# Top-k attention with a gated feed-forward layer on one core: token layout, zero matmuls and a reordered opening

## The chip, the cores and the metric

The kernel runs on one core of a Trainium2 chip. Its time is device time in microseconds (us). Three runs of the kernel before gave 1637.67, 1638.57 and 1638.79 us; the median, 1638.57 us, is the time before. One further execution was taken by the hardware profiler: 1636.0 us in all, of which the profile's span covers 1634.2 us. All steps below are read from that execution.

Engines are named as the profile names them: PE multiplies matrices (PEld is its weight load), DVE is the vector engine, ACT the scalar engine with its function tables, POOL the general-purpose engine, SP the engine that issues the DMAs. Each engine works through its own list of instructions in order.

## The reference

```python
# q, k, v: (8, 8, 576, 64)  batch, heads, tokens, head dim
scores = (1/sqrt(64)) * q @ k.T                    # 576 x 576 for each of 64 heads
kth    = 32nd largest of each row of scores
attn   = softmax(where(scores >= kth, scores, -1e9))
x      = (attn @ v), heads side by side            # 4608 x 512
h      = x @ w_in                                  # 512 -> 2048
out    = (h * sigmoid(1.702 h)) @ w_out            # 2048 -> 512
```

The two weight matrices arrive as 64-bit floats, so the kernel also has to turn them into 32-bit floats, piece by piece.

## The kernel before

**Tiling.** For one batch element a *slot* is 128 query rows of a pair of heads (or the 64 left-over rows of two pairs): 18 slots for each of the 8 batch elements, so N is 144. Per slot:

- `prepare` (L185) transposes the loaded q and k of a head pair on PE, and ACT copies them out; this happens once for each pair of heads of a batch element.
- `scores` (L215) multiplies q by k on PE, and ACT copies the 2 x 576 scores of each row to SBUF (tile `sc`, L232).
- `topk` (L234) finds the 32 largest on DVE: 14 operations, eight MAX8 (L241) and six MATCH_REPLACE8 (L244), two at a time for the two heads.
- `bounds` (L255) takes two small steps on POOL; `exponentials` (L263) takes two Prelu (L269) and two Exp steps (L271) on ACT; `divide` (L276) takes the reciprocal of the row sum on DVE. For slots below SETTLED (9) POOL writes diagonal matrices `by` (L286) with it; afterwards ACT and POOL scale the probabilities (L288, L289).
- `turn` (L291) transposes the probabilities on PE (L302, or L300 once settled; L305 for the left-over keys) with ACT copies `pt` (L310); `values` (L322) multiplies by v (L332), and ACT copies the result to `xT` (L344).
- When all four head pairs of a row tile are done, `hidden` (L364) makes a quarter of the hidden layer on PE (32 matmul instructions, L373), `tanh` (L385) runs on ACT, `gate` (L397) on DVE or POOL, and `project` (L411) multiplies by a quarter of w_out (8 matmul instructions of 512 columns, L421).

**Weights.** 32 pieces of 512 KB are loaded (`load_piece`, L113). `round_piece` (L122) turns each into 32-bit floats in steps: *size* on ACT (L142), *shift* on DVE (L143), *low* (L145) and *sign* (L144) on ACT, and *finish*, two POOL instructions (L138 and L139). `by_slot` (L442) says how many pieces each of slots 0 to 8 handles: 4, 3, 3, 4, 3, 4, 3, 4, 4. The finishes of one slot's pieces stand in POOL's list in the next slot.

**Order.** The order is written out by hand: the program text is the order on each engine. `slot(n)` (L469) runs topk of slot n beside the softmax and the values of slot n-1 and the scores of slot n+2. Slots -1 to 9 run through it, the later ones in pairs through `two_slots` (L554). In `slot`, shifts stand between the operations of topk (in slot 0 after operations 1, 2, 12 and 13, in other slots from operation 7 on). In slot 0 `prepare` and `scores(2)` stand behind topk and ahead of slot 1's exponentials. `project` runs from slot 7 on (n > PROJECTS, which is 6) when more than two gated groups wait in `to_project`; four buffers `gT` hold gated groups. `later` (`at`, L433) lists loads and preparations for each slot.

**Loads.** `load` (L156) puts token t*128 + p of a head into partition p, so each partition reads four pieces of 256 bytes for one head; `load_v` (L172) does the same for v, with one DMA for each head. q and k each have two buffers, raw weight pieces eight.

Of the kernel before, what the change touches and what calls it, by code (L numbers as in the profile page):

```python
# [11 lines left out]
F32 = mybir.dt.float32  # L12
# [4 lines left out]
P = 128  # L17
# [11 lines left out]
def kernel(  # L29
# [21 lines left out]

    nc = tc.nc

    B, H, S, D = q.shape
    C = H * D
    DFF = moe_w_in.shape[1]
    NP = H // 2
# [13 lines left out]
    SCALE = 1.0 / float(D) ** 0.5  # L73


    PROJECTS = 6
    SETTLED = 9
    assert D == 64 and 2 * TAIL == P and C == NP * P and C == PIECE and B % 2 == 0
    assert TOPK == 32 and NP == 4 and NF == 4 and NG == 4 and CC == 4
# [26 lines left out]
    wout = const.tile([P, FC, C], F32, name="wout")  # L106


    pieces = [(c, g) for g in range(NG - 1) for c in range(CC)] + [(None, f) for f in range(G)]
    pieces += [(c, NG - 1) for c in range(CC)] + [(None, f) for f in range(G, FC)]  # L110
    raw = {}

    def load_piece(n):  # L113
# [36 lines left out]
    qT, kT, vv = {}, {}, {}  # L150
    loaded = {}
    v_ends = [const.tile([P, 2, D], F32, name=f"v_e{i}") for i in range(6)]
    for t in v_ends:
        nc.gpsimd.memset(t[:], 0.0)

    def load(name, b, hp):  # L156
        src = q if name == "q" else k
        t = loads.tile([P, NF, 2, D], F32, name=f"{name}_l")
        for j in range(2):
            nc.sync.dma_start(  # L160
                t[:, :, j, :], src[b, 2 * hp + j, 0:FULL, :].rearrange("(t p) d -> p t d", p=P)
            )

        if name == "q":
            loaded["ends", b, hp] = loads.tile([P, 2, D], F32, name="ends")
        on = slice(0, TAIL) if name == "q" else slice(TAIL, P)
        nc.sync.dma_start(
            loaded["ends", b, hp][on, :, :], src[b, 2 * hp : 2 * hp + 2, FULL:S, :].rearrange("h p d -> p h d")
        )
        loaded[name, b, hp] = t  # L170

    def load_v(b, hp):  # L172
        main = vals.tile([P, NF, 2, D], F32, name="v_l")
        for j in range(2):
            nc.sync.dma_start(
                main[:, :, j, :], v[b, 2 * hp + j, 0:FULL, :].rearrange("(t p) d -> p t d", p=P)
            )


        tail = v_ends[(b * NP + hp) % len(v_ends)]  # L180
        for j in range(2):
            nc.sync.dma_start(tail[j * TAIL : (j + 1) * TAIL, j, :], v[b, 2 * hp + j, FULL:S, :])
        vv[b, hp] = main, tail
# [138 lines left out]
    def values(n):  # L322
        b, t, hps = slots[n]
        pt = st[n]["pt"]
        outs = []
        for p in range(2 if t == NF else 1):
            cols = slice(p * TAIL, (p + 1) * TAIL) if t == NF else slice(0, P)
            main, tail = vv[b, hps[p]]
            o = ps_t.tile([P, 512], F32, name="o", tag="tp")
            for c in range(NF + 1):  # L330
                for j in range(2):
                    nc.tensor.matmul(  # L332
                        o[j * D : (j + 1) * D, 0 : cols.stop - cols.start],
                        lhsT=main[:, c, j, :] if c < NF else tail[:, j, :],
                        rhs=pt[:, j * NF + c if c < NF else 2 * NF, cols],
                        start=(c == 0),
                        stop=(c == NF),
                    )
            outs.append((o, hps[p]))
        for o, hp in outs:  # L340
            if t < NF:
                if (b, t) not in xts:
                    xts[b, t] = xtp.tile([P, CC, P], F32, name="xT")
                nc.scalar.copy(out=xts[b, t][:, hp, :], in_=o[:, 0:P])  # L344
            else:
                if (b // 2, t) not in xts:
                    xts[b // 2, t] = xtt.tile([P, CC, P], F32, name="xT_t")
                at = b % 2 * TAIL
                nc.scalar.copy(out=xts[b // 2, t][:, hp, at : at + TAIL], in_=o[:, 0:TAIL])
        if hps[-1] == NP - 1:  # L350
            if t < NF:
                ready.append((xts.pop((b, t)), [(slice(0, P), b * S + t * P)]))
            elif b % 2:
                rows = [(slice(i * TAIL, (i + 1) * TAIL), (b - 1 + i) * S + FULL) for i in range(2)]
                ready.append((xts.pop((b // 2, t)), rows))
        st[n].clear()

# [53 lines left out]
    def project(blocks):  # L411

        if blocks[0] == 0:
            proj["on"] = to_project.pop(0)
            if proj["on"][1] == 0:
                proj["po"] = ps_p.tile([P, C], F32, name="po")
        gT, g, rows = proj["on"]
        po = proj["po"]
        for i in blocks:
            f = g * G + i  # L420
            nc.tensor.matmul(  # L421
                po[:], lhsT=gT[:, i, :], rhs=wout[:, f, :], start=(f == 0), stop=(f == FC - 1)
            )
        if blocks[-1] == G - 1 and g == NG - 1:
            ob = osp.tile([P, C], F32, name="ob")
            nc.scalar.mul(out=ob[:], in_=po[:], mul=0.5 / RAISE**2)
            for on, row in rows:
                nc.sync.dma_start(out[row : row + on.stop - on.start, :], ob[on, :])


    later = {}
# [1 line left out]
    def at(n, fn, *args):  # L433
        later.setdefault(n, []).append((fn, args))
# [4 lines left out]
    READY = (((-9, -8), (-7, -6), (-4, -3), (-2, -1)), ((-7, -6), (-4, -3), (-3, -2), (-1, -2)))  # L439
    FETCH = (((-13, -12), (-11, -10), (-7, -7), (-5, -4)), ((-11, -10), (-9, -8), (-5, -5), (-2, -2)))  # L440
    VALUES = ((-8, -7, 0, 0), (-8, -7, 2, 2))
    by_slot = dict(enumerate([4, 3, 3, 4, 3, 4, 3, 4, 4]))  # L442
    for n in by_slot:
        first = sum(map(len, list(by_slot.values())[:n]))
        by_slot[n] = list(range(first, first + by_slot[n]))
    assert by_slot[len(by_slot) - 1][-1] == NPIECE - 1
    for hp in range(NP):
        for name in "qk":
            at(max(hp - 2, -1), load, name, 0, hp)
            at(max(hp - 2, -1), prepare, name, 0, hp)  # L450
        if hp == 0:
            for x in by_slot[0][:2]:
                at(-1, load_piece, x)
    for hp in range(NP):
        at(hp - 1, load_v, 0, hp)
    for n in by_slot:
        for x in by_slot[n][0 if n else 2 :]:
            at(n - 1, load_piece, x)
    for b in range(1, B):
        for hp in range(NP):  # L460
            for i, name in enumerate("qk"):
# [4 lines left out]

    early = []

    def slot(n):  # L469
        nonlocal early  # L470
        todo = later.pop(n, [])
        for fn, args in todo:
            if fn is not prepare:
# [5 lines left out]
        if before:  # L479
            bounds(n - 1)  # L480
            exponentials(n - 1)
        if n < 0:
            for m in range(2):
                for args in preparing:
                    if args[2] == m:
                        prepare(*args)
                scores(m)
                if m == 0:
                    early = [round_piece(x) for x in by_slot[0][:2]]
                    for piece in early:  # L490
                        piece["size"]()
        some = early if n == 0 else []
        some = some + [round_piece(x) for x in by_slot.get(n, [])[len(some) :]]
        for piece in some[:2]:
            for step in ("low", "sign") if n == 0 else ("size",):
                piece[step]()
        if 0 <= n and not settled:
            if n > 0:
                for args in preparing:
                    prepare(*args)  # L500
                scores(n + 2)
        for piece in some[2:]:
            piece["size"]()
        shifts = [piece["shift"] for piece in some]
        tanh(aside)
        for i, op in enumerate(topk(n) if 0 <= n < N else [lambda: None] * 14):
            op()
            if i == 2 and unfinished:
                unfinished.pop(0)()
            if i == 5:  # L510
                if before:
                    divide(n - 1)
                while unfinished:
                    unfinished.pop(0)()
            if i == 8 and not aside:
                gate(aside)
            if (i in (1, 2, 12, 13) if n == 0 else i > 6) and shifts:
                shifts.pop(0)()
# [5 lines left out]
        if n == 0:  # L524
            for args in preparing:
                prepare(*args)
            scores(n + 2)
        for piece in some[2 if n == 0 else 0 : 2]:
            piece["low"]()
        going = settled and len(to_project) > (2 if n < N else 0)  # L530
        if going:
# [8 lines left out]
            piece["low"]()  # L540
        if before:
            values(n - 1)
        for i, piece in enumerate(some):
            if n or i > 1:
                piece["sign"]()
            unfinished.append(piece["finish"])
        if settled and n + 2 < N:
            scores(n + 2)
        if settled:
            for args in preparing[1:]:  # L550
                prepare(*args)
        hidden()

    def two_slots(n):  # L554
# [24 lines left out]
        def find(m):  # L579
            for i, op in enumerate(topk(m) if live(m) else [lambda: None] * 14):  # L580
                op()
                if i == 5 and live(m - 1):
                    divide(m - 1)

        def middle(m):
            go = going()
# [31 lines left out]
        hidden()  # L618

    with tc.manual_schedule():  # L620
        for n in range(-1, SETTLED + 1):
            slot(n)
        for n in range(SETTLED + 1, N + 1, 2):
            two_slots(n)
# [34 lines left out]
```

## Time and profile before

Time by stretch of the profiled execution. A stretch of the upper rows is one slot's topk on DVE, from its first MAX8 to that of the next slot.

| stretch, us | what runs on DVE | length | DVE busy | PE busy | ACT busy | POOL busy |
|---|---|---|---|---|---|---|
| 41.4 to 55.5 | slot 2, 3 shifts | 14.1 | 13.01 | 9.14 | 11.63 | 9.53 |
| 69.1 to 82.1 | slot 4, 3 shifts | 13.0 | 12.97 | 7.39 | 10.72 | 11.04 |
| 96.8 to 111.0 | slot 6, 3 shifts and a gate | 14.2 | 14.17 | 10.30 | 11.14 | 12.09 |
| 125.5 to 140.4 | slot 8, 4 shifts and a gate | 14.9 | 14.87 | 12.26 | 12.66 | 12.16 |
| 140.4 to 150.9 | slot 9, no shifts | 10.5 | 10.47 | 7.48 | 4.87 | 8.65 |
| 150.9 to 163.1 | slot 10 | 12.2 | 9.97 | 12.20 | 6.64 | 7.91 |
| 163.1 to 173.4 | slot 11 | 10.3 | 10.27 | 9.29 | 7.89 | 4.88 |
| 1580 to 1634 | end, no topk left | 54.0 | 4.46 | 50.69 | 10.82 | 1.73 |

The profiled execution took 1636.0 us, its span 1634.2 us, against a median of 1638.57 us. Busy time is summed over the engine's instructions; PE's overlap a little, so a full PE row means that no gap is left, not that the array is at its peak.

### The profile page before, as it was taken

Reading aid. Unit: us, or ns where it says so; the run is one execution under the profiler, and the core shown is the slowest. Engines: PE = TensorE matmul, PEld = TensorE weight load, DVE = VectorE, ACT = ScalarE, POOL = GpSimd, SP = SyncE. Lnnn points to the kernel's source line nnn. Section 1 sums busy time; section 2 is a strip of 40 time slices with the busy share of each in tenths; the row PEclk is TensorE's granted clock in tenths of the full one; section 3 lists DMA queues with packets and bytes.
Section 4 is the critical chain, followed back from the end, with each engine's and each line's share of the span. In section 5 each row is a group of like instructions: output and inputs, shape, how many; then the busy total and the mean of one; then the engine's idle time right before and its main releaser. Section 6 shows DMA issues by size and latency. Waiting matters only on the chain.

```text
span 1634.2 us, 31957 instructions
## 1 busy us (share of the span) xinstructions
PE 1576.2 (96%) x11923; PEld 1176.5 (72%) x11923; DVE 1489.5 (91%) x3211; ACT 1156.2 (71%) x2449; POOL 750.6 (46%) x783
## 2 busy tenths in 40 slices
PE   6578899999999999999999999999999999999999
PEld 4466677777777777777777777777777777777776
DVE  5999989999999999999999998999999999999960
ACT  6886777777777777777777777777777777777761
POOL 3777444444444444444444443444444444444430
PEclk9799999999999999999999999999999999999999
DMA  8342001110001001110000100111000100000000
GB/s 220 126 141 62 18 22 30 29 43 16 22 15 44 22 23 29 29 34 24 20 17 20 38 10 22 30 29 44 15 22 15 43 22 22 22 8 8 7 8 14
DMA packets 125723, 56.59 MB, mean 35 GB/s; under 512 B 116864, under 2 KB 116864, under 8 KB 125568
## 3 DMA queue, kind: packets, MB, share of 16 engines
q1 hardware_dynamic: 125568, 54.55, 12.7%
q8 instruction: 94, 1.54, 0.4%
q14 instruction: 61, 0.50, 0.1%
HBM read 45.09 MB, written 9.44 MB: 33 GB/s over the span
## 4 chain that ended last, share of the span: by engine, by line
PE 88%; DVE 7%; ACT 2%; POOL 1%; issue 1%; DMA 1%; SPq 0%; POOLq 0%; ACTq 0%
PE ph L373 30%; PE po L421 29%; PE s_ps L225 9%; PE o L332 9%; PE tp L300 8%; DVE top L241 3%; DVE left L244 2%; PE tp L193 2%; DVE wout L143 1%; ACT sc L232 1%; DVE win L143 1%; ACT pr L271 0%; POOL wout L138 0%; POOL wout L139 0%; DMA q_l<-in_q_dram 0%
## 5 line engine op out<-in xcount | busy, mean ns | idle before, releaser
L241 DVE MAX8 top<-left 128x8 f32<-128x576 f32 x864 | 610.2, 747 | 0.0
L421 PE MATMUL po<-wout,gT 128*128 128x512 f32 x1152 | 540.9, 593 | 0.0
L373 PEld LDWEIGHTS ph<-xT,win 128*128 128x128 f32 x4096 | 467.5, 192 | 41.7 <-issue 40.7
L373 PE MATMUL ph<-xT,win 128*128 128x128 f32 x4096 | 484.6, 277 | 0.0
L244 DVE MATCH_REPLACE8 left<-top,left 128x576 f32<-128x576 f32 x576 | 423.3, 742 | 0.0
L289 POOL TENSOR_SCALAR pr<-pr,rden 128x576 f32<-128x576 f32 x135 | 233.4, 1729 | 356.8 <-ACT th L390 352.7
L403 POOL TENSOR_SCALAR th<-th 128x512 f32<-128x512 f32 x133 | 199.0, 1496 | 224.2 <-ACT th L390 224.2
L310 ACT COPY pt<-tp 128x512 f32<-128x512 f32 (+1 forms) x432 | 193.2, 481 | 151.7 <-PE tp L300 141.8
L421 PEld LDWEIGHTS po<-wout,gT 128*128 128x128 f32 x1152 | 197.5, 191 | 142.0 <-issue 141.8
L269 ACT ACTIVATE sc<-sc,cut 128x576 f32<-128x576 f32 x288 | 208.1, 773 | 127.9 <-POOL cut L260 127.9
L232 ACT COPY sc<-s_ps 128x576 f32<-128x576 f32 x288 | 169.9, 644 | 79.4 <-PE s_ps L225 79.1
L300 PEld LDWEIGHTS tp<-ident,pr 128*128 128x128 f32 x1215 | 145.3, 141 | 108.7 <-issue 59.2
L271 ACT ACTIVATE pr<-sc,low 128x576 f32<-128x576 f32 x288 | 219.1, 763 | 0.0
L244 DVE MATCH_REPLACE8 left<-top,sc 128x576 f32<-128x576 f32 x288 | 211.7, 743 | 0.0
L241 DVE MAX8 top<-sc 128x8 f32<-128x576 f32 x288 | 202.0, 743 | 10.5 <-ACT sc L232 10.5
L225 PE MATMUL s_ps<-k_t,q_t 64*128 64x288 f32 (+1 forms) x1280 | 184.4, 435 | 1.2 <-ACT k_t L195 1.2
L300 PE MATMUL tp<-ident,pr 128*128 128x128 f32 x1215 | 177.2, 273 | 5.0 <-ACT pt L310 4.0
L404 POOL TENSOR_TENSOR gT<-th,h 128x512 f32<-128x512 f32 x133 | 169.8, 1277 | 11.1
L332 PE MATMUL o<-pt,v_l 128*64 128x128 f32 (+1 forms) x2560 | 158.3, 267 | 1.7 <-ACT pt L310 0.9
L332 PEld LDWEIGHTS o<-pt,v_l 128*64 128x64 f32 x2560 | 131.3, 138 | 31.8 <-ACT pt L310 16.3
L225 PEld LDWEIGHTS s_ps<-k_t,q_t 64*128 64x128 f32 (+1 forms) x1280 | 101.0, 179 | 59.9 <-issue 40.9
L260 POOL TENSOR_SCALAR cut<-top 128x2 f32<-128x2 f32 x144 | 32.5, 226 | 220.3 <-DVE top L241 220.3
(50 smaller groups left out, 1171.0 us busy)
## 6 DMA issues: line engine op xcount, KB each, us to landing
q_l<-in_q_dram SPq DMA_DIRECT2D x64, 128.0 KB, 2.6
k_l<-in_k_dram SPq DMA_DIRECT2D x64, 128.0 KB, 2.6
raw<-in_moe_w_in_dram SPq DMA_DIRECT2D x16, 512.0 KB, 4.3
v_l<-in_v_dram SPq DMA_DIRECT2D x64, 128.0 KB, 2.6
raw<-in_moe_w_out_dram SPq DMA_DIRECT2D x16, 512.0 KB, 3.6
out_dram<-ob SPq DMA_DIRECT2D x32, 256.0 KB, 2.1
ends<-in_q_dram SPq DMA_DIRECT2D x32, 32.0 KB, 2.4
ends<-in_k_dram SPq DMA_DIRECT2D x32, 32.0 KB, 2.4
```

The lines of the kernel that those rows point to most:

```text
L225: nc.tensor.matmul(ps[i][rows, c, 0:HALF], lhsT=qT[b, hps[p]][on, cols], rhs=kT[b, hps[p]][on, FIRST[i] + c * HALF : FIRST[i] + (c + 1) * ...
L241: nc.vector.max(top[:, i, 8 * r : 8 * r + 8], (left if r else sc)[:, i, :])
L244: nc.vector.match_replace(left[:, i, :], top[:, i, 8 * r : 8 * r + 8], (left if r else sc)[:, i, :], LOWEST)
L269: nc.scalar.activation(sc[:, i, :], sc[:, i, :], AF.Prelu, bias=cut[:, i : i + 1], alpha=HUGE)
L271: nc.scalar.activation(pr[:, i * S : (i + 1) * S], sc[:, i, :], AF.Exp, bias=low[:, i : i + 1], accum_out=den[:, i : i + 1],)
L289: nc.gpsimd.tensor_scalar(pr[:, S : 2 * S], pr[:, S : 2 * S], rden[:, 1:2], None, op0=ALU.mult)
L300: nc.tensor.transpose(tp[:, c * P : (c + 1) * P], pr[:, at], ident[:])
L310: nc.scalar.copy(out=to, in_=tp[:, 0 : blocks * P])
L332: nc.tensor.matmul(o[j * D : (j + 1) * D, 0 : cols.stop - cols.start], lhsT=main[:, c, j, :] if c < NF else tail[:, j, :], rhs=pt[:, j * N ...
L373: nc.tensor.matmul(ph[:, i, :], lhsT=win[:, c, f * P : (f + 1) * P], rhs=xT[:, c, :], start=(c == 0), stop=(c == CC - 1),)
L403: nc.gpsimd.tensor_scalar(th[:], th[:], 1.0, None, op0=ALU.add)
L421: nc.tensor.matmul(po[:], lhsT=gT[:, i, :], rhs=wout[:, f, :], start=(f == 0), stop=(f == FC - 1))
```

## The change

Five edits, taken from the diff:

1. **Token layout.** q, k and v are loaded with four adjacent tokens in a partition (token 4p + t); the output rows follow the same pattern. v's tile is laid out by head, and one DMA loads both heads.
2. **Matmuls of zeros.** `stay_warm` issues matmuls whose result nobody reads: seven at the start on a tile of zeros (cleared by DVE), and four on the identity at one or two places in each of slots 0 to 7.
3. **Opening.** Slot -1 becomes `opening`: q and k of two head pairs are loaded before any weight piece, and then the rest of q, k and the first v. Preparation and scores stand ahead of topk in slot 0, which ends after its topk and shifts, so that slot 1's exponentials come next on ACT.
4. **Shifts behind each topk.** All of a slot's shifts stand after its 14 operations.
5. **Pieces.** All of w_in is handled before w_out; slots 0 to 9 take 2, 2, 3, 3, 3, 3, 4, 4, 4, 4 pieces, and PROJECTS becomes 7. The last four finishes fall into the first `two_slots`.

```diff
-    PROJECTS = 6
+    PROJECTS = 7
...
+    def stay_warm(count, of=ident[:]):
+        none = ps_p.tile([P, C], F32, name="none", tag="po")
+        for i in range(count):
+            nc.tensor.matmul(none[:, 0:P], lhsT=of, rhs=of, start=True, stop=True)
...
-                t[:, :, j, :], src[b, 2 * hp + j, 0:FULL, :].rearrange("(t p) d -> p t d", p=P)
+            nc.sync.dma_start(t[:, :, j, :], src[b, 2 * hp + j, 0:FULL, :].rearrange("(p t) d -> p t d", t=NF))
...
+        main = vals.tile([P, 2, NF, D], F32, name="v_l")
+        nc.sync.dma_start(
+            main[:].rearrange("p j t d -> p j (t d)"),
+            v[b, 2 * hp : 2 * hp + 2, 0:FULL, :].rearrange("j (p t) d -> p j (t d)", t=NF),
+        )
...
-    by_slot = dict(enumerate([4, 3, 3, 4, 3, 4, 3, 4, 4]))
+    by_slot = dict(enumerate([2, 2, 3, 3, 3, 3, 4, 4, 4, 4]))
...
+    def opening():
+        stay_warm(7, v_ends[0][:].rearrange("p j d -> p (j d)"))
+        for hp in range(2):
+            for name in "qk":
+                load(name, 0, hp)
+        for x in by_slot[0]:
+            load_piece(x)
+        for m in range(2):
+            for name in "qk":
+                prepare(name, 0, m)
+            if m == 1:
+                early.extend(round_piece(x) for x in by_slot[0])
+                for piece in early:
+                    piece["size"]()
+            scores(m)
+        for hp in range(2, NP):
+            for name in "qk":
+                load(name, 0, hp)
+        load_v(0, 0)
+        for x in by_slot[1]:
+            load_piece(x)
...
+        if not settled:
+            for args in preparing:
+                prepare(*args)
+            scores(n + 2)
+            stay_warm(4)
...
-            if (i in (1, 2, 12, 13) if n == 0 else i > 6) and shifts:
-                shifts.pop(0)()
+        for piece in some:
+            piece["shift"]()
+            unfinished.append(piece["finish"])
+        if n == 0:
+            return
...
+        if not ready and not settled:
+            stay_warm(4)
         hidden()
...
             for i, op in enumerate(topk(m) if live(m) else [lambda: None] * 14):
                 op()
                 if i == 5 and live(m - 1):
                     divide(m - 1)
+                if i > 1 and unfinished:
+                    unfinished.pop(0)()
```

More of the change, by code (lines that the diff above doesn't have):

```diff
@@ L106 @@
     wout = const.tile([P, FC, C], F32, name="wout")
-    pieces = [(c, g) for g in range(NG - 1) for c in range(CC)] + [(None, f) for f in range(G)]
-    pieces += [(c, NG - 1) for c in range(CC)] + [(None, f) for f in range(G, FC)]
+    pieces = [(c, g) for g in range(NG) for c in range(CC)] + [(None, f) for f in range(FC)]
     raw = {}
@@ L152 @@
     v_ends = [const.tile([P, 2, D], F32, name=f"v_e{i}") for i in range(6)]
-    for t in v_ends:
-        nc.gpsimd.memset(t[:], 0.0)
+    for i, t in enumerate(v_ends):
+        (nc.gpsimd if i else nc.vector).memset(t[:], 0.0)
+    def stay_warm(count, of=ident[:]):
+        none = ps_p.tile([P, C], F32, name="none", tag="po")
+        for i in range(count):
+            nc.tensor.matmul(none[:, 0:P], lhsT=of, rhs=of, start=True, stop=True)
     def load(name, b, hp):
@@ L159, in load @@
         for j in range(2):
-            nc.sync.dma_start(
-                t[:, :, j, :], src[b, 2 * hp + j, 0:FULL, :].rearrange("(t p) d -> p t d", p=P)
-            )
+            nc.sync.dma_start(t[:, :, j, :], src[b, 2 * hp + j, 0:FULL, :].rearrange("(p t) d -> p t d", t=NF))
         if name == "q":
@@ L172, in load_v @@
     def load_v(b, hp):
[L173 to L177, printed above, removed]
+        main = vals.tile([P, 2, NF, D], F32, name="v_l")
[3 more added lines that the diff above has]
+        )
         tail = v_ends[(b * NP + hp) % len(v_ends)]
@@ L333, in values @@
                         o[j * D : (j + 1) * D, 0 : cols.stop - cols.start],
-                        lhsT=main[:, c, j, :] if c < NF else tail[:, j, :],
+                        lhsT=main[:, j, c, :] if c < NF else tail[:, j, :],
                         rhs=pt[:, j * NF + c if c < NF else 2 * NF, cols],
@@ L351, in values @@
             if t < NF:
-                ready.append((xts.pop((b, t)), [(slice(0, P), b * S + t * P)]))
+                to = out[b * S : b * S + FULL, :].rearrange("(p t) c -> p t c", t=NF)[:, t, :]
+                ready.append((xts.pop((b, t)), [(slice(0, P), to)]))
             elif b % 2:
-                rows = [(slice(i * TAIL, (i + 1) * TAIL), (b - 1 + i) * S + FULL) for i in range(2)]
+                first = [(b - 1 + i) * S + FULL for i in range(2)]
+                rows = [(slice(i * TAIL, (i + 1) * TAIL), out[x : x + TAIL, :]) for i, x in enumerate(first)]
                 ready.append((xts.pop((b // 2, t)), rows))
@@ L426, in project @@
             nc.scalar.mul(out=ob[:], in_=po[:], mul=0.5 / RAISE**2)
-            for on, row in rows:
-                nc.sync.dma_start(out[row : row + on.stop - on.start, :], ob[on, :])
+            for on, to in rows:
+                nc.sync.dma_start(to, ob[on, :])
     later = {}
@@ L446 @@
     assert by_slot[len(by_slot) - 1][-1] == NPIECE - 1
-    for hp in range(NP):
-        for name in "qk":
[L449 to L458, printed above, removed]
+    for n in range(2, len(by_slot)):
+        for x in by_slot[n]:
+            at(n - 1, load_piece, x)
+        if n < NP + 1:
+            at(n - 1, load_v, 0, n - 1)
+    for hp in range(2, NP):
+        for name in "qk":
+            at(hp - 2, prepare, name, 0, hp)
     for b in range(1, B):
@@ L467 @@
     early = []
+    def opening():
[13 more added lines that the diff above has]
+            scores(m)
+        for hp in range(2, NP):
+            for name in "qk":
[3 more added lines that the diff above has]
+            load_piece(x)
     def slot(n):
-        nonlocal early
         todo = later.pop(n, [])
@@ L481, in slot @@
             exponentials(n - 1)
[L482 to L504, printed above, removed]
+        some = [round_piece(x) for x in by_slot.get(n, [])] if n else early
+        if n == 0:
+            for piece in some:
+                piece["low"]()
+                piece["sign"]()
+        else:
+            for piece in some[:2]:
+                piece["size"]()
+        if not settled:
[3 more added lines that the diff above has]
+            stay_warm(4)
+        if n > 0:
+            for piece in some[2:]:
+                piece["size"]()
         tanh(aside)
-        for i, op in enumerate(topk(n) if 0 <= n < N else [lambda: None] * 14):
+        for i, op in enumerate(topk(n) if n < N else [lambda: None] * 14):
             op()
@@ L516, in slot @@
                 gate(aside)
-            if (i in (1, 2, 12, 13) if n == 0 else i > 6) and shifts:
-                shifts.pop(0)()
+        for piece in some:
+            piece["shift"]()
+            unfinished.append(piece["finish"])
+        if n == 0:
+            return
         if aside:
@@ L523, in slot @@
                 prepare(*args)
[L524 to L528, printed above, removed]
+        for piece in some[:2]:
             piece["low"]()
@@ L542, in slot @@
             values(n - 1)
[L543 to L546, printed above, removed]
+        for piece in some:
+            piece["sign"]()
         if settled and n + 2 < N:
@@ L620 @@
     with tc.manual_schedule():
-        for n in range(-1, SETTLED + 1):
+        opening()
+        for n in range(SETTLED + 1):
             slot(n)
```

## The prediction

> **What bounds the kernel now.** I read the page's shares and chain of waits first, then a table of windows cut at the slots (the start of each slot's first MAX8), then the timeline of the first 200 us.
>
> ```profile
> PE 1576.2 (96%) x11923; PEld 1176.5 (72%) x11923; DVE 1489.5 (91%) x3211; ACT 1156.2 (71%) x2449; POOL 750.6 (46%) x783
> ...
> PE 88%; DVE 7%; ACT 2%; POOL 1%; issue 1%; DMA 1%; SPq 0%; POOLq 0%; ACTq 0%
> ```
>
> ```profile
> 0.00:10.50 10.50, 4.89 (x17) 3.32 (x17) 0.00 (x0) 3.44 (x8) 1.56 (x12) 1.00 0.70 187
> 10.50:22.30 11.80, 7.31 (x26) 4.92 (x26) 11.09 (x24) 8.42 (x19) 0.15 (x1) 1.00 1.00 215
> 22.30:41.40 19.10, 13.35 (x64) 9.73 (x65) 13.37 (x26) 14.19 (x32) 12.11 (x12) 1.00 0.87 242
> 111.00:125.50 14.50, 12.17 (x92) 8.98 (x92) 14.47 (x29) 12.65 (x25) 9.38 (x10) 1.00 0.48 156
> ```
>
> ```profile
> 200.00:1580.00 1380.00, 1379.33 (x10671) 1030.38 (x10670) 1306.25 (x2846) 994.81 (x2122) 630.57 (x650) 1.00 0.10 24
> ```
>
> Columns: stretch, length, busy PE, PEld, DVE, ACT, POOL, granted clock, DMA share, GB/s. From 200 to 1580 us PE has 0.67 us of gaps: PE is the bound, and its order there is untouched. Before that DVE is: 14.47 of 14.5 us busy in slot 7. The chain's 7% DVE lies there. So the change can win only what it takes off the road to slot 12 (first MAX8 at 173.37), after which both programs run the same list at PE's pace.
>
> **The parts.** A topk without shifts or gate takes 9.9 us with its divide (slot 4: 12.9 us, less three shifts of 1.46, 0.77 and 0.76 net); a gate on DVE adds 0.66.
>
> *Opening.* DVE starts at 10.55, behind scores that PE runs slowly:
>
> ```profile
> 7.55 2.50 PE L225 MATMUL s_ps<-k_t,q_t 64*128 64x288 f32 x8 [0.47 <-ACT k_t L195]
> ...
> 41.69 1.24 PE L225 MATMUL s_ps<-k_t,q_t 64*128 64x288 f32 x8
> ```
>
> The same eight matmuls take half at 41.69. The granted clock reads 1.00 in both places; I believe the durations. Seven zero matmuls are 14 instructions of 0.236 us (L302's 3.78 us for 16, cold), about 0.9 to 4.2 us: they end before k lands (5.78), so they delay nothing. If PE is then fast: 1.26 us on the scores, some 0.4 on k's transposes. Ends 0 and -1.9; I take **-1.2**, nearer the gain, since the busy stretch that starts at 32.88 was fast again by 40.45. DVE starts at 9.35.
>
> *Slot 0.* 11.75 us held four shifts and a wait of 0.67. Two uncontended shifts (0.41 each, 0.33 net) give 9.65 + 0.7 = 10.35: **-1.4**.
>
> *Slot 1*, 19.1 us, is where most goes. DVE waited 4.79 us for den:
>
> ```profile
> 31.28 0.17 DVE L280 TENSOR_SCALAR some<-den 128x2 f32<-128x2 f32 x1 [4.79 <-ACT pr L271]
> ```
>
> ACT reached slot 0's exponentials only at 28.30 (topk was done at 22.3), behind preparation, score copies and weight steps whose q came late (PE waited 11.5 us for q in four waits, DMA share 1.0). Then three shifts waited for sizes and POOL. Now q and k of four pairs come ahead of all but two pieces on SP's queue (some 1.8 us of issue a tensor: k of the fourth pair issued by 16.5), and those steps stand ahead of topk. Following ACT: two pieces issued at 8.1 to 9.1 plus 4.3 us to land let sizes end near 14, then scores copy 1.1, low and sign 2.4, preparation 1.8, scores copy 1.5: exponentials start at 21, den (3.0 us later) at 24 against DVE's divide at 19.7 + 4.2 = 23.9. Slot 1 is 9.9 + 0.7 + 0.1 of wait = 10.7: **-8.4**. v is hidden: its first matmul stood at 40.45, here near 29, its load issued near 18.
>
> *Slots 2 to 9.* What a shift costs depends on POOL:
>
> ```profile
> 12.94 0.41 DVE L143 TENSOR_SCALAR win<-win 128x512 uint32<-128x512 uint32 x1
> ...
> 88.09 1.53 DVE L143 TENSOR_SCALAR win<-win 128x512 uint32<-128x512 uint32 x1
> ...
> 88.04 1.29 POOL L138 TENSOR_TENSOR wout<-wout,raw 128x512 int32<-128x512 int32 x1
> 89.42 1.36 POOL L139 TENSOR_TENSOR wout<-wout,raw 128x512 f32<-128x512 f32 x1
> ```
>
> A shift that starts 0.05 us after a POOL instruction ends 0.29 us after it. The Trainium skill ("SBUF — State Buffer", Who interferes with whom) says why and speaks against this edit: vector and POOL share a port pair, the first holds it for its whole instruction, and the other blocks. By slot 0's row four shifts behind topk cost 4 x 0.33 = 1.3 us; by the rule, with POOL always queued, each waits for one POOL instruction: 4 x 1.35 = 5.4. What decides is when POOL is done. Its list in a slot: bounds 0.42, one finish 2.6, `by` 1.2 (after rden, at 4.4), the other finishes at 2.6: with three pieces it ends at 5.6 + 5.3 = 10.9, as topk does (9.9 to 10.6); with four at 13.6. So slots 2 to 6 pay about a row's price plus one wait, slots 7 to 9 the rule's, cut off when POOL runs dry: 14.4 us each. Slots 3, 4, 5, 6: 12.4, 11.9, 12.3, 12.6. Slot 2 is 10.9 plus 2.3 us for den, since ACT is still late from the opening (10.7 us of ACT work in slot 1 puts den at 36.9, DVE's need at 34.6). Sum 13.2 + 49.2 + 43.2 = 105.6 against 109.5 (41.42 to 150.91): **-3.9**. Ends: row price everywhere and no ACT wait, -10; every shift a full wait, +6.
>
> ACT itself allows this: slot 7 with four pieces took 14.54 us with 1.45 idle, so 13.1.
>
> *Zero matmuls in slots 0 to 7.* PE idles there; eight warm ones are 1.0 us. They pay only if PE stays fast:
>
> ```profile
> 47.84 3.79 PE L302 MATMUL tp<-by,pr 128*128 128x128 f32 x16 [4.91 <-POOL by L286]
> ...
> 130.76 2.05 PE L302 MATMUL tp<-by,pr 128*128 128x128 f32 x16 [2.64 <-POOL by L286]
> ```
>
> A gap of 4.91 us costs the next 16 matmuls 1.7 us, one of 2.64 nothing. In the new order the zeros stand right before and behind the scores, leaving about 4.4 us until `by`: likely still slow. Either way ACT has 1 us of slack before den is needed: **0**, ends -1 and +2.
>
> *Slots 10 and 11.* Four finishes now stand in slot 10 on POOL, ahead of L289, the POOL gate (2.8) and bounds(10): 0.2 + 7.9 + 1.7 + 2.65 + 2.8 = 15.3 us, where topk is done at 10. Queued behind them: bounds(10), so the exponentials, so den at 18.8, against DVE's need at 14.2 in slot 11: a stall of 4.6. Slot 10 loses its old stall of 2.2 (12.2 us there). 10.0 + 14.6 against 22.5: **+2.1**, ends 0 and +4.
>
> *One project later.* 8 x 0.43 = 3.5 us of PE work leaves slot 7. Comparing the two PE lists: before leaves out one project in slots 12 and 13 (too few groups waiting), the new program does it there, and the lists are alike after. PE idles there:
>
> ```profile
> 187.18 0.48 PE L300 MATMUL tp<-ident,pr 128*128 128x128 f32 x1 [4.01 <-ACT pt L310]
> ```
>
> So **0**; +3.5 if that gap is gone.
>
> *Layout.* v falls from 1024 packets of 256 bytes to 256 of 1 KB; q and k still land in 256-byte pieces. After 30 us the DMA share is under 0.8 and loads run slots ahead: 0. Output rows stay 2 KB.
>
> Sum: -1.2 - 1.4 - 8.4 - 3.9 + 2.1 = **-12.8 us**: 1636.0 becomes 1623.2, and the median 1638.57 (2.6 above the profiled run) 1625.8; I say 1626.
>
> **Rivals.** *A, the above*: 62%, own range 1619 to 1633.
> *B, shifts never wait*: POOL done in time, ACT not late, warm PE; slots 2 to 9 give -10: 1638.6 - 18.9 = 1620. For it: POOL is at most 85% busy before. Against: 2.6 us a finish. 26%.
> *C, the wait only moves*: each shift waits a full POOL instruction in all slots, +6 instead of -3.9: 1636. For it: the 1.53 us row. Against: POOL idles before bounds in slots of three pieces (3.5 us at 96.97). 7%.
> *D, slower*: one more group waits in `to_project` for good (three left after a project, not two), with four `gT` buffers; a gate that finds its buffer still being read blocks POOL, then L289, then PE's transposes. At 0.4 us for each of 67 pairs it is 27 us: 1653. It decides once a gate arrives before the project of its buffer's old group has ended. Now a gate writes at 808.69, the project two places back ended at 801.7: 7 us of room. 5%.
>
> **Chances.** A change under 0.2% (3.3 us) can't be told from none. Faster 0.89 (A and B, and part of C), same 0.06, slower 0.05. Range 1616 to 1635: B's best end to A's worst, leaving out part of C and D.
>
> **What would show it.** Slot 1 about 10.7 us; shifts of 0.4 us in slots 0 and 1, over 1 us in slots 7 to 9; a DVE wait at L280's counterpart of over 4 us in slot 11; first MAX8 of slot 12 near 161; PE without gaps from about 190. If slot 12 comes early and the end doesn't, the PE stretch grew, and I am wrong.

## The result, and the profile after

| | before | after |
|---|---|---|
| median of four runs, us | 1638.34 | 1631.99 |
| lowest to highest, us | 1637.67 to 1638.79 | 1630.02 to 1632.40 |
| profiled execution (span), us | 1636.0 (1634.2) | 1632.4 (1630.6) |

The changed kernel is faster: the ratio is 0.9959 with an interval of 0.9942 to 0.9976, or -6.35 us by the medians against the -12.8 that the sum gave. Right in direction, half in size. The two profiled executions differ by only -3.6 us, because before's is faster than all four of its runs and after's is as slow as the slowest; the accounts below are made on these two, and small differences between single traces carry that spread. One part of it can be seen: the kernel with only the layout changed (below), profiled at 1637.69 us, has a wait of 1.47 us in slot 12 that before's trace lacks.

First the page of the changed kernel: its busy shares, and its chain of waits by engine.

```profile
PE 1584.6 (97%) x12025; PEld 1184.1 (73%) x12025; DVE 1479.2 (91%) x3212; ACT 1155.9 (71%) x2449; POOL 754.1 (46%) x782
...
PE 88%; ACT 5%; DVE 4%; POOL 1%; issue 1%; SPq 0%; DMA 0%; POOLq 0%; ACTq 0%
```

DVE has 10.3 us less to do (1489.5 before), and its share of the chain fell from 7 to 4%. But ACT's rose from 2 to 5%. That is the result in one line: shifts got cheaper, and DVE now waits longer for ACT.

Then the table of windows of the changed kernel, cut at its slots (first MAX8 to first MAX8; here the opening, slots 0, 1, 2, 8 and 11), and below it the long stretch. Columns as before: stretch, length, busy PE, PEld, DVE, ACT, POOL, granted clock, DMA share, GB/s.

```profile
0.00:10.61 10.61, 7.59 (x33) 6.06 (x34) 0.17 (x1) 3.48 (x8) 1.42 (x11) 0.88 0.54 116
10.61:20.93 10.32, 5.55 (x29) 3.90 (x29) 10.32 (x23) 8.00 (x19) 0.49 (x1) 0.83 0.87 217
20.93:33.00 12.07, 9.60 (x42) 7.50 (x40) 10.64 (x26) 8.55 (x19) 7.08 (x9) 0.64 0.93 334
33.00:49.19 16.19, 12.54 (x111) 10.61 (x111) 10.98 (x27) 12.16 (x26) 7.42 (x9) 0.93 0.35 113
113.62:128.12 14.50, 11.64 (x89) 8.57 (x88) 14.47 (x28) 12.59 (x25) 12.17 (x12) 1.00 0.53 166
...
152.52:168.56 16.04, 8.31 (x34) 4.57 (x34) 10.06 (x23) 7.62 (x16) 10.33 (x11) 0.68 0.07 22
```

```profile
200.00:1576.40 1376.40, 1375.27 (x10641) 1026.82 (x10640) 1302.92 (x2839) 993.44 (x2119) 627.67 (x647) 1.00 0.09 24
```

Compare the length of a row with its DVE column. In slot 1, 1.43 us are missing, in slot 2 5.21, in slot 11 5.98: waits. In slot 8 nothing is missing: shifts fill it. From 200 us on PE is full, as before. In both kernels the span ends 1398.0 us after slot 18's first MAX8 (236.18 before, 232.58 after). So in these two traces nothing was won or lost behind slot 18, and all accounts can be made in the first 18 slots:

| stretch | before, us | after, us | change | forecast |
|---|---|---|---|---|
| opening (to the first MAX8) | 10.55 | 10.61 | +0.1 | -1.2 |
| slot 0 | 11.75 | 10.32 | -1.4 | -1.4 |
| slot 1 | 19.12 | 12.07 | -7.1 | -8.4 |
| slot 2 | 14.07 | 16.19 | +2.1 | -0.9 |
| slots 3 to 9 | 95.42 | 93.42 | -2.0 | -3.0 |
| slots 10 and 11 | 22.46 | 25.95 | +3.5 | +2.1 |
| slots 12 to 17 | 62.81 | 64.02 | +1.2 | 0 |

All shifts together took 32.9 us of DVE before and 20.8 after (-12.1). DVE's waits of over 0.3 us in slots 0 to 17 came to 12.1 us before and 19.0 after (+6.9); all of them are for ACT.

### The profile page after: what moved, and what is told of

Its sections match the earlier page's. It is cut to its first block, busy times and chain, and to the rows that moved or that the text cites. A ratio compares the mean times of both kernels' runs of the same rounds, so it can differ in the third digit from the quotient of the medians.

```text
span 1630.6 us, 32137 instructions
## 1 busy us (share of the span) xinstructions
PE 1584.6 (97%) x12025; PEld 1184.1 (73%) x12025; DVE 1479.2 (91%) x3212; ACT 1155.9 (71%) x2449; POOL 754.1 (46%) x782
## 2 busy tenths in 40 slices
DMA packets 100636, 56.61 MB, mean 35 GB/s; under 512 B 83584, under 2 KB 91776, under 8 KB 100480
## 3 DMA queue, kind: packets, MB, share of 16 engines
q1 hardware_dynamic: 100480, 54.55, 12.1%
q8 instruction: 95, 1.56, 0.4%
## 4 chain that ended last, share of the span: by engine, by line
PE 88%; ACT 5%; DVE 4%; POOL 1%; issue 1%; SPq 0%; DMA 0%; POOLq 0%; ACTq 0%
PE ph L381 30%; PE po L429 29%; PE o L338 9%; PE s_ps L231 9%; PE tp L306 8%; DVE top L247 2%; DVE left L250 2%; PE tp L199 1%; ACT sc L238 1%; ACT pr L277 1%; ACT raw L146 1%; PE tp L308 1%; DVE wout L145 0%; ACT sc L275 0%; DMA raw<-in_moe_w_in_dram 0%
## 5 line engine op out<-in xcount | busy, mean ns | idle before, releaser
L338 PEld LDWEIGHTS o<-pt,v_l 128*64 128x64 f32 x2560 | 131.6, 138 | 31.3 <-ACT pt L316 15.8
L266 POOL TENSOR_SCALAR cut<-top 128x2 f32<-128x2 f32 x144 | 38.2, 265 | 208.5 <-DVE top L247 206.8
```

The costliest lines, as they stand in the source:

```text
L338: nc.tensor.matmul(o[j * D : (j + 1) * D, 0 : cols.stop - cols.start], lhsT=main[:, j, c, :] if c < NF else tail[:, j, :], rhs=pt[:, j * N ...
```

## The experiments

Each was compared with runs of the kernel before on the same chip (medians 1637.58 to 1637.76 us). Diffs are against the changed kernel unless another is named.

### Shifts back between the operations of topk

```diff
+        shifts = [piece["shift"] for piece in some]
...
+            if i > 6 and shifts:
+                shifts.pop(0)()
         for piece in some:
-            piece["shift"]()
```

> In slots 1 to 9 the shifts go back between the operations of topk, from operation 7 on, and in slot 0 as well; all else as in the changed kernel. Theory (a shift pays for the POOL instruction that runs when it is issued, so behind topk, where POOL has often finished, it is cheaper): the shifts of a slot of three cost about 3 us again instead of 1.0 to 2.0, those of a slot of four 4 us, and the time rises by 5 to 9 us, to 1637 to 1641. Rival (POOL has the same number of instructions to run and DVE meets them wherever the shifts stand): within 2 us of 1632.

Measured: 1637.78 us, ratio 1.0001 (0.9992 to 1.0010). Without the shifts' new place the change gains nothing: the place is worth 5.8 us by the two medians (6.5 when each is taken against its own runs of before). All shifts took 34.7 us instead of 20.8. Of those 13.9 us only 5.2 reached slot 18, mainly because DVE, when it is faster, waits more for ACT (19.0 us against 12.3 in all). That nothing is left of the change does not mean that its other parts do nothing: in this trace slots 0 to 2 are still 6.2 us shorter than before, but slots 3 to 9, which now have more pieces, are 3.8 us longer, and slots 10 to 12, with the finishes that moved there, 4.7. The new opening by itself was not tried.

The timelines show why a group of shifts is cheaper. First DVE's timeline of the changed kernel in slots 6 and 7 (start, length, then what, and the number of instructions drawn together):

```profile
97.64 1.41 DVE L145 TENSOR_SCALAR wout<-wout 128x512 uint32<-128x512 uint32 x4
...
110.33 3.37 DVE L145 TENSOR_SCALAR wout<-wout 128x512 uint32<-128x512 uint32 x4
```

And POOL's timeline of the same kernel at those two places:

```profile
97.81 1.32 POOL L266 TENSOR_SCALAR cut<-top 128x2 f32<-128x2 f32 x1 [0.25 <-DVE top L247]
...
110.01 1.30 POOL L140 TENSOR_TENSOR wout<-wout,raw 128x512 int32<-128x512 int32 x1
111.38 1.36 POOL L141 TENSOR_TENSOR wout<-wout,raw 128x512 f32<-128x512 f32 x1
```

At 97.64 POOL had run dry, and four shifts in a row took 1.41 us. It is POOL's small `cut`, 0.22 us elsewhere, that takes 1.32 there: it started 0.17 us after the shifts and ended with them. At 110.33 POOL was in the middle of a finish, and four took 3.37.

### The same edit alone, in the kernel before

The shifts of each slot, slot 0's four too, stand behind topk; nothing else is changed.

```diff
-            if (i in (1, 2, 12, 13) if n == 0 else i > 6) and shifts:
-                shifts.pop(0)()
+        for shift in shifts:
+            shift()
```

> The kernel before with only the shifts of every slot, slot 0's too, put behind topk. Theory (the shifts behind topk are worth about 6 us wherever POOL is done in time, with nothing else changed): 1631 to 1634 us, slots of three pieces under 13.2 us. Rival (they pay only with the changed order of pieces and the opening; with 4, 3, 3, 4, 3, 4, 3, 4, 4 pieces POOL is never done in time): 1636 to 1639, shifts of four at 3.4 us or more, of three at 3.

Measured: 1635.15 us, ratio 0.9983 (0.9977 to 0.9990): between the two. Four shifts took 1.50 us in slot 5, where POOL was dry, but 3.70 in slot 8 and 3.67 in slot 0; three took 4.40 in slot 4 (POOL had four finishes from slot 3) and 4.22 in slot 1. All shifts together took 29.4 us, against 32.9 before and 20.8 in the changed kernel. In the kernel before the edit is worth 2.6 us, in the changed one 5.8. The rival has a part of the truth: POOL has to be done in time, and with the old list it seldom is.

### Shifts where POOL waits

Nine slots of pieces (2, 3, 3, then 4 each). Only a slot's first shift stands behind topk; the others stand in the next slot ahead of `divide`, where POOL itself waits for the divide.

```diff
+            if i == 5:
+                while shifts:
+                    shifts.pop(0)()
...
-        for piece in some:
-            piece["shift"]()
+        for i, piece in enumerate(some):
+            if i == 0:
+                piece["shift"]()
+            else:
+                shifts.append(piece["shift"])
```

> Nine slots, with only the first shift behind topk; the others stand in the next slot ahead of the divide, where POOL waits for the divide's result. Theory (a shift costs what POOL is busy with at that moment, and POOL is idle there): those shifts take 0.4 us each, slots of four pieces fall from 14.5 us to 13.0 to 14.0 (then set by POOL's own 13.6 us), six such slots give -3 to -6 us against nine slots alone: 1625 to 1628 us. Rival (the shift's place doesn't matter, since POOL needs the sizes it makes and falls late by as much): slots of four stay at 14.5 us and the time at 1630 to 1632.

Measured: 1624.75 us, ratio 0.9922 (0.9908 to 0.9937), 6 us less than nine slots alone (below). DVE's timeline of this kernel in slots 6 and 7:

```profile
102.01 0.73 DVE L145 TENSOR_SCALAR wout<-wout 128x512 uint32<-128x512 uint32 x1
106.77 1.08 DVE L145 TENSOR_SCALAR wout<-wout 128x512 uint32<-128x512 uint32 x3
107.92 0.17 DVE L286 TENSOR_SCALAR some<-den 128x2 f32<-128x2 f32 x1
```

Three shifts ahead of the divide take 1.08 us, about 0.36 each, as in slot 0. In slots 5 and 9 POOL was still in a finish there, and three took 2.2. Slots 3 to 9 together took 91.3 us, against 96.4 with nine slots alone. The two traces differ at slot 18 by only 2.2 us, since slot 2's wait is 5.40 us here and 2.47 there, where PE was faster (more on this below). The theory held: a shift costs what POOL is doing at that moment.

### No zero matmuls

```diff
     def stay_warm(count, of=ident[:]):
+        return
```

> All zero matmuls are left out; their results are read by nobody, so the output is the same. Theory (the zeros stand in slot 1 on the road: eight of them took 2.07 us at the slow rate between scores(3) and the transposes of slot 0, which had been free to start 4.8 us earlier): the DVE wait for den in slot 2 falls from 5.18 to about 3 us, and the time by about 2 us, to 1630. Rival (the zeros keep PE fast and shorten slots 2 to 7): the 16 transposes of a slot go back from 2.05 to 3.7 us in slots 5 to 7 and the time rises by 1 to 3 us, to 1633 to 1635.

Measured: 1631.25 us, ratio 0.9959 (0.9944 to 0.9974), as with them. Slot 2's wait falls from 5.18 to 3.69 us; slot 2 is shorter by 1.5 us and slot 3 longer by 1.3. In this place and number the zeros are worth nothing.

### The old layout of tokens

```diff
-            nc.sync.dma_start(t[:, :, j, :], src[b, 2 * hp + j, 0:FULL, :].rearrange("(p t) d -> p t d", t=NF))
+            nc.sync.dma_start(t[:, :, j, :], src[b, 2 * hp + j, 0:FULL, :].rearrange("(t p) d -> p t d", p=P))
```

(v and the output rows likewise.)

> The token layout of before is put back (q, k, v loads, v's tile and the output rows), all else as in the changed kernel. Theory (the layout is no gain; it makes SP's first issues longer, 1.37 and 1.28 us for q's and k's pairs of DMAs against 0.99 and 1.14, so that k lands later): DVE's first MAX8 comes 0.3 to 0.6 us earlier than 10.61 and the time falls by 0 to 1 us. Rival (the layout is where part of the gain comes from, by a fifth fewer packets): q and k of pairs 1 to 3 land later, slot 1 and slot 2 grow, and the time rises by 2 us or more.

Measured: 1630.20 us, ratio 0.9950 (0.9933 to 0.9967), which overlaps the changed kernel's interval. DVE starts at 10.85, not earlier than 10.61 as the theory had it: k's transposes began 0.4 us sooner, but took 1.09 us instead of 0.63. Slot 1, though, has no wait and takes 10.76 us.

And the new layout alone, in the kernel before:

> The kernel before, with only the adjacent-token layout of q, k, v and of the output rows. Theory (the layout is no gain: q and k still land in 256-byte pieces, and putting the old layout back in the changed kernel cost nothing): 1638 to 1640 us, q's transposes of slots 1 and 2 still waiting for q as in the profile before. Rival (fewer packets bring q, k and v earlier in the first 30 us): 1636 or less, with PE's four waits for q in slots 0 to 2 (11.5 us in all) cut to under 9.

Measured: 1637.68 us, ratio 1.0002 (0.9993 to 1.0011). With a fifth fewer packets (125723 before, 100636 after) the layout gains nothing.

### Nine slots of pieces instead of ten

```diff
-    by_slot = dict(enumerate([2, 2, 3, 3, 3, 3, 4, 4, 4, 4]))
+    by_slot = dict(enumerate([2, 3, 3, 4, 4, 4, 4, 4, 4]))
```

> The 32 pieces are spread over slots 0 to 8 (2, 3, 3, 4, 4, 4, 4, 4, 4), so the last four finishes stand in slot 9 and none in slot 10. Theory (the POOL queue in slot 10, four finishes ahead of the gate and bounds, costs the waits of 4.30 us in slot 11 and 1.65 and 1.90 us in slot 12): these waits go, a wait of about 2.2 us appears in slot 10 as before the change, slot 12 starts 4 to 5 us earlier and the time falls by 3 to 5 us, to 1627 to 1629. Rival (the waits of slots 11 and 12 have another cause, or PE is the bound there and only waits elsewhere): within 1 us of 1632.

Measured: 1630.78 us, ratio 0.9957 (0.9942 to 0.9972). The stalls of slots 11 and 12 (4.30 + 3.55 us) are gone, and 2.21 us are back in slot 10, as before; while the pieces moved forward cost something: slots 9 to 12 together are 9.5 us shorter, slots 3 to 8 7.0 us longer. The time from the first MAX8 to slot 18's is 218.47 us against 221.97. Of these 3.5 us 2.5 belong to slots 3 to 12, and so to the list. The rest lies in slots 0 to 2, where PE was faster in this execution (scores(3) took 1.50 us against 2.54). The medians differ by only 1.2 us, within the spread of four runs.

With the old layout as well:

> Nine slots (2, 3, 3, then four pieces each) and the old layout of tokens. Theory (the two gains are separate: no stall in slots 11 and 12, and no wait in slot 1): 1628 to 1629 us, first MAX8 of slot 18 near 227.5. Rival (both only buy the same slack in slots 1 and 2): 1630.5, as each alone.

Measured: 1627.60 us, ratio 0.9941 (0.9926 to 0.9955). All four runs (1627.12 to 1629.34) are below all four of the changed kernel, so the two edits together gain, by the medians 4.4 us. How much is due to each stays open: neither alone is clear of the spread, slot 1 still has a wait of 1.56 us, and this trace reaches slot 18 only 0.5 us before that of nine slots alone.

### More zeros in the opening

```diff
             for name in "qk":
                 prepare(name, 0, m)
+                if m == 0:
+                    stay_warm(4 if name == "q" else 2)
```

> The changed kernel, with four more zero matmuls behind q's transposes of the first pair and two behind k's, so that PE has no gap over 1 us from the first zero to scores(0). Theory (PE was slow again at scores(0) because of the gap before them): scores(0) take 1.3 us instead of 2.50, the first MAX8 comes at 9.3 to 9.7 instead of 10.6, and the end moves by up to -1 us. Rival (fast or slow in the opening isn't set by the gap, or the zeros delay k's transposes): scores(0) still 2.5 us, first MAX8 at 10.5 to 11.5, the end the same or 1 us later.

Measured: 1630.89 us, ratio 0.9958 (0.9943 to 0.9973). PE's timeline of the changed kernel in the opening (in brackets the idle time before, and what ended it):

```profile
1.03 3.35 PE L162 MATMUL none<-v_e 128*128 128x128 f32 x14 [1.03 <-DVE v_e L156]
4.50 0.65 PE L199 MATMUL tp<-ident,q_l 128*128 128x128 f32 x4
6.46 0.63 PE L199 MATMUL tp<-ident,k_l 128*128 128x128 f32 x4 [1.31 <-DMA k_l<-in_k_dram]
...
7.77 2.50 PE L231 MATMUL s_ps<-k_t,q_t 64*128 64x288 f32 x8 [0.56 <-ACT k_t L201]
```

And of this experiment:

```profile
6.50 0.63 PE L199 MATMUL tp<-ident,k_l 128*128 128x128 f32 x4
6.96 0.27 PE L205 MATMUL tp<-ident,ends 128*128 128x128 f32 x1
7.07 0.61 PE L162 MATMUL none<-ident 128*128 128x128 f32 x4
7.81 1.45 PE L231 MATMUL s_ps<-k_t,q_t 64*128 64x288 f32 x8
```

In the changed kernel q's transposes were fast, k's too, then scores(0) slow again. With the gaps filled scores(0) were fast and DVE started at 9.76 instead of 10.61; but scores(1), behind gaps of 0.74 and 0.58 us, took 2.34. All three kernels that filled these gaps had fast scores(0). Of the seven profiles with only the first seven calls of zeros here, two did: with nine slots, after a gap of 0.94 us ahead of k's transposes, and with nine slots and the old layout (0.65). With the old layout alone scores(0) were slow after 0.83, so that gap's length alone doesn't decide; what does stays open. Those 0.85 us are within the spread of the medians.

### Scores(3) out of slot 1

```diff
-        if not settled:
-            for args in preparing:
+        if n == 1:
+            held = preparing
+        elif not settled:
+            for args in held if n == 2 else preparing:
                 prepare(*args)
-            scores(n + 2)
+            scores(n + 1 if n == 2 else n + 2)
             stay_warm(4)
...
+        if n == 2:
+            for args in preparing:
+                prepare(*args)
+            scores(n + 2)
```

> The changed kernel, with scores(3) and their preparation moved from slot 1 (ahead of slot 0's transposes on PE, and without the eight zero matmul instructions there) to slot 2, behind its exponentials. Theory (slot 2's wait of 5.18 us comes from ACT waiting for transposes that stand behind slow scores and zeros on PE): transposes of slot 0 start at 28 instead of 33, the wait falls under 2 us, and the end comes 2 to 4 us sooner: 1628 to 1630 us. Rival (ACT has that work to do anyway and is only late elsewhere): the wait moves to slot 3, slots 2 and 3 together stay near 28.3 us, the time 1631 to 1632.

Measured: 1633.62 us, ratio 0.9975 (0.9964 to 0.9986). The transposes began at 27.50 and slot 2's wait was gone, but slot 3's is 6.59 us: slots 2 and 3 are 29.9 us together against 28.3. The wait only moved, as the rival had it, and the median is 1.6 us above the changed kernel's, outside what either expected.

### Four edits together, and PE kept warm

Nine slots, old layout, late shifts and the filled opening together (the diffs above):

> Nine slots, old layout of tokens, shifts in the next slot ahead of the divide, and the zeros that fill the opening. Theory (the gains are separate): first MAX8 at 9.3, slot 2's wait 2.6 us as with nine slots and the old layout (5.4 with late shifts alone), so slot 18 starts near 222 and the median is 1620 to 1622 us. Rival (late shifts take the slack that the other two buy, or POOL sets the slots of four): 1624 to 1625, as late shifts alone.

Measured: 1624.16 us, ratio 0.9917 (0.9902 to 0.9931), the fastest median of all, but no better than late shifts alone by more than the spread; DVE waits 3.99 us in slot 2. Into this kernel went more zeros in slots 0 and 1:

```diff
+        stay_warm(11)
         for hp in range(2, NP):
...
-                prepare(*args)
+                prepare(*args, fill=(4, 14)[n] if n < 2 else 0)
             scores(n + 2)
-            stay_warm(4)
+            if n != 1:
+                stay_warm(4)
```

(`fill` zeros stand in `prepare` ahead of the last transpose of k.)

> The last kernel (nine slots, old layout, late shifts, filled opening), with zero matmuls also where PE idles in slots 0 and 1: eleven behind scores(1), four and fourteen ahead of the last transposes of the preparations in slots 0 and 1, none behind scores(3). The granted clock read 0.50 to 0.60 from 15 to 25 us there. Theory (ACT is late in slots 1 and 2 because it waits for a PE that has turned slow in its gaps): granted clock 1.00 from 5 to 40 us, scores(2) and scores(3) 1.25 us each instead of 2.69 and 1.50, transposes of slot 0 at 2.05 instead of 2.98, the waits of slots 1 and 2 fall from 1.79 + 3.99 to under 3 together, median 1621 to 1622 us. Rival (ACT's own work and its waits for the weights' transfers make it late): waits of slots 1 and 2 stay at 5 us or more, median 1624 or later.

Measured: 1624.88 us, ratio 0.9929 (0.9916 to 0.9943). The table of windows of the changed kernel in steps of 5 us, then that of this experiment:

```profile
20.00:25.00 5.00, 4.99 (x19) 3.96 (x19) 5.00 (x11) 3.07 (x9) 3.35 (x4) 0.50 0.74 195
...
30.00:35.00 5.00, 5.00 (x23) 4.24 (x21) 5.00 (x11) 2.38 (x5) 2.83 (x4) 0.50 1.04 393
```

```profile
20.00:25.00 5.00, 5.00 (x44) 4.65 (x42) 4.96 (x13) 4.03 (x8) 2.94 (x4) 1.00 0.55 162
...
30.00:35.00 5.00, 3.78 (x43) 3.17 (x42) 5.00 (x12) 4.41 (x11) 1.76 (x3) 1.00 1.02 339
35.00:40.00 5.00, 3.06 (x24) 2.27 (x22) 0.60 (x5) 5.00 (x11) 1.30 (x1) 1.00 0.40 133
```

The granted clock is 1.00 where it was 0.50, and 44 matmuls fit where 19 did (many are zeros). Slot 1's wait is gone and slot 2 starts at 30.42, but there DVE waits 4.37 us: from 35 to 40 us ACT has no gap and DVE works 0.60 us. So both theories hold a part. Between the den (the row sums that the Exp steps leave for the divide) of slot 0 and that of slot 1, ACT waits 1.5 us for PE, against 2.9 in the kernel without these zeros; but 1.66 us of waits for weights' transfers are there instead, and ACT's own work stays, and so does the time. Since the zeros behind scores(3) are gone too, PE's speed and the length of its queue are not told apart here.

## Why the prediction was half right

**What held.** The bound (PE from slot 18 on, nothing gained there), slot 0 to 0.03 us, and the rule of shifts: cheap where POOL is dry (0.75 us for two in slot 0), a part of a POOL instruction each where it is not. Slots 3 to 6 took 49.8 us against 49.2, slots 7 to 9 43.6 against 43.2. Zeros in the slots and the layout at nothing, and no trouble from the `gT` ring, held too. Case B (shifts never wait) fell with slots 7 to 9, where four took 3.4 to 4.1 us, case C with slots 3 to 6, and of case D there is no sign: PE's stretch behind slot 18 has its old length.

The forecasts of the stretches promised 9.2 us more gain than the two traces show. By the medians 6.45 us are missing; the other 2.8 lie within the spread of single executions.

**Slots 1 and 2: ACT's waits were counted too low** (1.4 + 3.0 us). The prediction put exponentials(0) at 21, slot 0's den at 24 and slot 1's at 36.9, with "10.7 us of ACT work in slot 1". The work was right, the waits were not. ACT's timeline of the changed kernel:

```profile
13.84 0.66 ACT L144 ACTIVATE win<-raw 128x512 f32<-128x512 f32 x1 [1.02 <-DMA raw<-in_moe_w_in_dram]
15.16 0.66 ACT L144 ACTIVATE win<-raw 128x512 f32<-128x512 f32 x1 [0.65 <-DMA raw<-in_moe_w_in_dram]
...
22.45 1.18 ACT L238 COPY sc<-s_ps 128x576 f32<-128x576 f32 x2 [1.85 <-PE s_ps L231]
...
30.98 1.18 ACT L238 COPY sc<-s_ps 128x576 f32<-128x576 f32 x2 [2.00 <-PE s_ps L231]
...
34.94 0.59 ACT L316 COPY pt<-tp 128x512 f32<-128x512 f32 x1 [1.64 <-PE tp L308]
36.07 0.75 ACT L316 COPY pt<-tp 128x512 f32<-128x512 f32 x2 [0.54 <-PE tp L308]
38.09 0.27 ACT L350 COPY xT<-o 128x128 f32<-128x128 f32 x1 [1.27 <-PE o L338]
```

Exponentials(0) began at 23.5 instead of 21. The first step that failed is the transfers: issued from 8.8 us on, the first two pieces landed at 13.8 and 15.2, and their sizes were done at 15.8 instead of 14. The wait of 1.85 us for scores(2) came on top. From slot 0's den (26.5) to slot 1's (42.3) are 15.9 us, of which the last four brackets are 5.45 us of waits, so 10.4 of work. The prediction's own times leave 12.9 us there, 2.2 more than the work it names, without saying for what. DVE's timeline shows what came of it, in slot 1 and in slot 2:

```profile
26.51 0.17 DVE L286 TENSOR_SCALAR some<-den 128x2 f32<-128x2 f32 x1 [1.39 <-ACT pr L277]
...
42.36 0.17 DVE L286 TENSOR_SCALAR some<-den 128x2 f32<-128x2 f32 x1 [5.18 <-ACT pr L277]
```

PE was late because it was cold and does things in order. Its timeline in the changed kernel:

```profile
28.66 2.54 PE L231 MATMUL s_ps<-k_t,q_t 64*128 64x288 f32 x8 [0.16 <-ACT k_t L201]
31.13 2.07 PE L162 MATMUL none<-ident 128*128 128x128 f32 x8
32.99 3.04 PE L308 MATMUL tp<-by,pr 128*128 128x128 f32 x16
```

`by` was there at 28.2, but scores and zeros at half speed stood ahead of the transposes, which so began 4.8 us later. How much of that is speed and how much the queue was not separated; without the zeros slot 2's wait was 3.69. The trace of nine slots bears the reading out. PE happened to be fast there from 28 us on: scores(3) took 1.50 us and the 16 transposes 1.95, ACT waited 1.45 us for PE between the two dens, and slot 2's wait was 2.47, although its list has a third piece in slot 1 (1.9 us of ACT). With nine slots and late shifts PE was slow (2.69 and 2.81), and ACT waited 4.03 and DVE 5.40. The last experiment made PE fast by intent, and ACT waited 1.5 us; the time did not fall, with the transfers late by 1.66. Whether the list of two pieces would be faster with a warm PE was not tried.

**The opening** (1.3 us). The step "if PE is then fast" was taken near the gain. It was fast for q and k and not for scores(0). Filling the gaps gave 0.85 of the 1.2 us in its trace.

**Slots 10 to 17** (2.6 us). POOL's queue was right: bounds(10) was put 15.3 us behind the start of slot 10 and came after 15.15 (at 157.76). Here is the time that ACT waited for it and, from DVE's timeline, DVE's own waits:

```profile
158.02 1.44 ACT L275 ACTIVATE sc<-sc,cut 128x576 f32<-128x576 f32 x2 [10.09 <-POOL cut L266]
```

```profile
161.01 0.17 DVE L286 TENSOR_SCALAR some<-den 128x2 f32<-128x2 f32 x1 [4.30 <-ACT pr L277]
168.56 1.42 DVE L247 MAX8 top<-sc 128x8 f32<-128x576 f32 x2 [1.65 <-ACT sc L238]
174.66 0.17 DVE L286 TENSOR_SCALAR some<-den 128x2 f32<-128x2 f32 x1 [1.90 <-ACT pr L277]
```

The first was forecast (4.6). What was left out is what stands behind: ACT had waited 10.09 us, PE then 7.73 us for ACT, so scores(12) and den of slot 11 were late as well, 3.55 us more. The prediction priced one stall and let the chain be on time afterwards. The nine-slot experiment has none of the three waits.

**Rivals.** The outcome lies in case A (1619 to 1633), with its mechanism; the waits were more, the shifts as said.

## What to carry over

A time for an engine's list is its work plus its waits for the others at the speed they have there: list the waits, and take a cold PE's durations where PE idles. When two engines hold each other up, look for the moment at which one of them must wait for the other's result, and put the work that suffers there; here this was worth 6 us. A stall that is priced once has followers: walk one slot further on each engine that it held.

## What the hardware showed

The granted clock reads 1.00 in the first 45 us of the kernel before, with scores(0) at 2.50 us, and in the changed kernel, whose zeros had made PE fast once, 0.50 from 20 to 25 us with scores(2) at 2.69. In the kernel kept warm, 1.00 stands with 1.49. So in these traces the reading 1.00 at the start, ahead of its first change, says nothing; the durations do.

A DVE shift does not only wait for POOL: POOL's 0.22 us `cut` took 1.32 beside four shifts in a row that had begun 0.17 us before it. In both cases the one that came first held the other up.
